# Turning half of one batch's heads by DMA instead of TensorE, and two small edits at the start, in a fused attention and GeGLU kernel

## Chip, cores, metric

One core of one Trainium2 chip. The metric is the device time of one execution in microseconds (us). The runs of one kernel in one job lay within 0.2 to 1.0% of each other; medians and ranges are given.

## The reference, cut to what matters

Inputs and output are float32; the kernel computes in bf16.

```python
B, H, S, Nb, D = 8, 8, 576, 16, 64
k_all = concat([beacon_k, k], axis=2); v_all = concat([beacon_v, v], axis=2)   # 592 keys
scores = q @ k_all.T / sqrt(D), causal over the 576, the 16 beacons always seen
attn   = softmax(scores) @ v_all
x = attn.transpose(0, 2, 1, 3).reshape(4608, 512)
out = (gelu(x @ w_gate) * (x @ w_val)) @ w_out        # d_ff = 1536
```

## The kernel before

It works batch by batch. Its score matmuls read queries and keys with the head dimension on the partitions (the tile `qkT`, one slot for each of four head pairs), while the inputs have tokens in rows, so it turns every batch. There are two ways in the kernel:

- **Packed and turned on TensorE** (batches 0 and 1): a load puts six consecutive tokens of a head into one partition (`qk6`), and 25 small transposes per head pair turn them.
- **Token rows and turned by DMA** (batches 2 to 7): the loads put one token into one partition (`q_sb`, `k_sb`), and ten DMA transposes, issued by SyncE, write `qkT`. TensorE does nothing for them.

All loads into bf16 tiles are issued by GpSimd and cast on the way. GpSimd also makes the causal masks of batches 1 to 7. It takes loads and masks in the order of the program: in the changed kernel batch 1's first mask starts at 60.20 us, behind the loads ahead of it, and at 48.86 with those loads moved (changed_q2_loads_later).

```python
    def load_qk6(b, h0, h1, ws=(1, 0)):                 # packed
        for w in ws:
            src = (q, k)[w]
            dma(qk6_of(b)[0][0:96, w, h0:h1, :],
                src[b, h0:h1, :, :].rearrange("h (p r) d -> p h (r d)", r=6))

    def transpose_pe(b, m, by_act=False):               # packed, on TensorE
        t_ps = psum_s.tile([P, 2, 1024], BF16, name="t_ps", tag="s")
        for w in range(2):
            tr_part(b, m, w, t_ps[:, w, :])             # 12 transposes, and 1 for the beacons
        ...                                             # copies to qkT

    def transpose_half(b, m, w, by_act=False):          # batch 0: q and k in two PSUM tiles
        ...
        if by_act:
            act(out_ap, in_ap, ACT.Copy)
        else:
            keep(nc.vector.tensor_copy(out_ap, in_ap))

    def transpose_dma(b):                               # token rows, by DMA
        q_sb, k_sb = q_ring[b % NRING], k_ring[b % NRING]
        for j in range(5):
            for w, src, n, c in (...q..., ...k...):
                keep(nc.sync.dma_start_transpose(
                    out=qkT[:, :, w, c + j * P : c + j * P + n],
                    in_=src[0:n, j, :, :].rearrange("p h d -> p (h d)")))
    # [cut]
    load_qk6(1, 0, 4)                                   # the order of the loads
    load_kb(1)
    load_gate_val(8, 12)
    load_qk6(1, 4, H)
    for f0 in (0, 4, 8):
        load_out_w(f0, f0 + 4)
    load_v(1)
    loads = qk_loads(2)
    ...
    ahead(5)                                            # batch 2's queries: before batch 1's masks
    # [cut] batch 0's scores; then, per batch b >= 1:
            o(4)                                        # output matmuls of the batch before
            scores(b, (0, 0)); scores(b, (0, 2)); scores(b, (0, 1))
            o(5)
            if b == 1:
                transpose_pe(1, 3)
            ahead(2)                                    # two loads, between masks
            o(4)
            scores(b, (0, 3), (1, 3)); scores(b, (1, 0)); scores(b, (1, 2))
            ahead(2)
            o(5)
            av(b, 0)                                    # attend: values of pair 0
```

The softmax here doesn't subtract the row's maximum and nothing guards it: scores larger than these inputs give would overflow.

## Time and profile before

| what | value |
|---|---|
| time, median of four runs | 369.48 us (368.95 to 369.69) |
| TensorE busy, granted clock | 97% of the span, 0.999 |
| third output-weight load landed | 45.53 us |
| last value load of batch 1 landed | 49.51 us |
| first gate matmul of batch 0, of batch 1 | 21.99 and 65.40 us: a stage of 43.41 us |

The landings are read off the trace, each DMA from the start of its issue to the semaphore update that tells of its landing.

The page of the kernel before. First come the span and the busy time of each engine, then rows of 40 equal slices of the span (a digit is the busy share in tenths), and engine shares of the chain that ended last.

```profile
span 367.6 us, 7553 instructions
PE 356.4 (97%) x3046; PEld 182.5 (50%) x3096; DVE 150.7 (41%) x256; ACT 188.1 (51%) x243; POOL 159.3 (43%) x282
PE   7799999999999999999999999999999999999996
PEclk9999999999999999999999999999999999999999
DMA  7999999999299915993399929992791130000112
PE 88%; DMA 5%; ACT 2%; issue 2%; POOL 1%; DVE 1%; ACTq 0%; POOLq 0%
```

PE (TensorE) is full (97%) and at full clock (0.999). But for the first quarter of the span the DMA engines are full as well: slices 2 to 10, up to about 90 us, are all 9. Up to 49.5 us they are busy with loads that batches 0 and 1 need.

The timeline of PE before, with start, length, instruction group and, in brackets, the idle time before it and what ended it.

```profile
16.61 0.27 PE L172 MATMUL s_ps<-qkT 64*128 64x208 bf16 x2 [0.41 <-ACT expT L175]
41.79 0.70 PE L180 MATMUL t_ps<-eye,qk 96*64 96x96 bf16 x24
46.04 1.02 PE L172 MATMUL o_ps<-wo_sb,hT_sb 128*128 128x512 bf16 x4
48.90 0.70 PE L180 MATMUL t_ps<-eye,qk 96*64 96x96 bf16 x24
51.61 1.25 PE L172 MATMUL o_ps<-wo_sb,hT_sb 128*128 128x512 bf16 x5
52.70 1.08 PE L172 MATMUL x_ps<-v_sb,expT 128*128 128x65 bf16 x30
```

The two groups of 24 transposes (41.79 and 48.90) are what the change takes away. Output matmuls (`o_ps`) and the first attend of batch 1 (softmax weights times values, `x_ps` at 52.70) start without a wait: the weights and the values were there, the latter with 3.2 us to spare.

The timeline of GpSimd (POOL) before, around batch 1's first masks.

```profile
45.81 3.31 POOL L108 DMA_DIRECT2D q_sb<-in_q_dram  x4 [1.67 <-DMA wo_sb<-in_moe_w_out_dram]
49.10 0.77 POOL L298 TENSOR_SCALAR_AFFINE_SELECT expT<-expT 128x224 bf16<-128x224 bf16 x2
```

GpSimd waits for the landing of an output-weight load before it issues a query load of batch 2. In this trace a load that waits starts 0.3 us after the landing of the one eight places ahead of it: the last value load of batch 1 at 40.73 and the first two query loads of batch 2 at 43.27 and 45.81, after the three output-weight landings at 40.44, 42.98 and 45.53. The masks come behind these loads.

### The profile page before, as it was taken

To read this page: it belongs to the slowest core of one execution; us is meant where nothing else is said; L and a number is where in the kernel's file an instruction comes from. 1 tells how busy PE (TensorE), PEld (TensorE's weight loads), DVE (VectorE), ACT (ScalarE), POOL (GpSimd) and SP (SyncE) were. 2 spreads that over 40 slices of the span, in tenths; PEclk is the share of its full clock that TensorE was granted. 3 is DMA by queue.
4 is the path that set the end of the run, shared out by engine and by line. 5 is a ranking of instruction groups with operands and counts; after the bars stand their busy time and mean duration, and the time that the engine had idled before them with its cause. 6 is when DMAs were issued, how large, how long until landed. Compare 5 with 4: busy or idle time off the path is not lost.

```text
span 367.6 us, 7553 instructions
## 1 busy us (share of the span) xinstructions
PE 356.4 (97%) x3046; PEld 182.5 (50%) x3096; DVE 150.7 (41%) x256; ACT 188.1 (51%) x243; POOL 159.3 (43%) x282
## 2 busy tenths in 40 slices
PE   7799999999999999999999999999999999999996
PEld 7564445544554455444544455445544554444443
DVE  4454543543353334433443235433444254333322
ACT  3963578237743576348723873367534863321210
POOL 8934397942495247723684249504700430000000
PEclk9999999999999999999999999999999999999999
DMA  7999999999299915993399929992791130000112
GB/s 104 177 203 204 194 143 115 148 145 109 63 114 149 135 46 118 148 153 49 90 142 136 106 61 135 156 99 67 113 132 37 41 108 1 2 0 29 59 38 105
DMA packets 149858, 38.35 MB, mean 104 GB/s; under 512 B 136384, under 2 KB 145344, under 8 KB 149824
## 3 DMA queue, kind: packets, MB, share of 16 engines
q0 software_dynamic: 104848, 19.11, 69.1%
q1 hardware_dynamic: 44976, 18.76, 28.0%
q8 instruction: 24, 0.39, 0.4%
q14 instruction: 10, 0.08, 0.1%
HBM read 38.27 MB, written 9.44 MB: 130 GB/s over the span
## 4 chain that ended last, share of the span: by engine, by line
PE 88%; DMA 5%; ACT 2%; issue 2%; POOL 1%; DVE 1%; ACTq 0%; POOLq 0%
PE gv_ps L172 42%; PE o_ps L172 25%; PE x_ps L172 7%; PE s_ps L172 7%; DMA q_sb<-in_q_dram 3%; DMA qkT<-k_sb 2%; ACT expT L175 2%; PE y_ps L180 2%; PE v_ps L172 1%; PE g_ps L172 1%; PE t_ps L180 1%; PE w_ps L172 1%; POOL v_sb L108 1%; DVE qkT L217 0%; DVE qkT L199 0%
## 5 line engine op out<-in xcount | busy, mean ns | idle before, releaser
L175 ACT ACTIVATE ge_sb<-gv_ps 128x512 bf16<-128x512 f32 x101 | 59.4, 597 | 132.8 <-PE gv_ps L172 132.8
L423 DVE TENSOR_TENSOR hT_sb<-gv_ps,ge_sb 128x512 bf16<-128x512 f32 x101 | 69.1, 690 | 105.0 <-ACT ge_sb L175 102.6
L175 ACT ACTIVATE expT<-s_ps 128x960 bf16<-128x960 f32 (+3 forms) x112 | 99.7, 968 | 19.5 <-PE s_ps L172 18.4
L172 PE MATMUL gv_ps<-xT_sb,wg_sb 128*128 128x512 bf16 x400 | 107.8, 379 | 0.2
L172 PE MATMUL gv_ps<-xT_sb,wv_sb 128*128 128x512 bf16 x390 | 104.1, 379 | 0.4
L172 PE MATMUL o_ps<-wo_sb,hT_sb 128*128 128x512 bf16 (+2 forms) x413 | 100.7, 374 | 2.5 <-issue 1.3
L298 POOL TENSOR_SCALAR_AFFINE_SELECT expT<-expT 128x256 bf16<-128x256 bf16 (+2 forms) x140 | 51.7, 385 | 97.9 <-ACT expT L175 97.5
L172 PEld LDWEIGHTS <-wv_sb 128*128 128x128 bf16 x432 | 42.2, 98 | 50.7
L172 PEld LDWEIGHTS <-wg_sb 128*128 128x128 bf16 x432 | 41.1, 98 | 46.7
L172 PEld LDWEIGHTS <-hT_sb 128*128 128x128 bf16 x444 | 38.8, 98 | 43.4 <-issue 6.2
L442 DVE COPY o_sb<-o_ps 128x512 f32<-128x512 f32 (+2 forms) x37 | 25.0, 675 | 42.1 <-PE o_ps L172 42.0
L108 POOL DMA_DIRECT2D v_sb<-in_v_dram x40 | 33.7, 862 | 6.3 <-DMA wg_sb<-in_moe_w_gate_dram 2.4
L172 PEld LDWEIGHTS <-expT 128*128 128x128 bf16 (+1 forms) x960 | 32.5, 97 | 6.7 <-POOL expT L298 1.6
L172 PE MATMUL s_ps<-qkT 64*128 64x512 bf16 (+5 forms) x384 | 32.4, 281 | 3.3 <-DVE qkT L221 1.6
L108 POOL DMA_DIRECT2D k_sb<-in_k_dram x30 | 25.2, 842 | 22.1 <-DMA q_sb<-in_q_dram 15.1
L172 PE MATMUL x_ps<-v_sb,expT 128*128 128x65 bf16 x930 | 33.3, 194 | 0.0
L108 POOL DMA_DIRECT2D q_sb<-in_q_dram x30 | 25.3, 885 | 4.3 <-DMA wo_sb<-in_moe_w_out_dram 3.5
L349 DVE TENSOR_TENSOR y_sb<-x_ps,r_sb 128x640 bf16<-128x640 f32 x31 | 25.6, 824 | 1.3 <-DVE r_sb L347 0.3
L172 PEld LDWEIGHTS <-qkT 64*128 64x128 bf16 x384 | 14.0, 94 | 24.2 <-issue 15.7
L347 DVE RECIPROCAL r_sb<-x_ps 128x10 f32<-128x10 f32 x31 | 6.8, 221 | 36.6 <-PE x_ps L172 36.6
L382 DVE COPY xT_sb<-y_ps 128x576 bf16<-128x576 bf16 x15 | 6.9, 457 | 10.6 <-PE y_ps L180 10.6
L597 ACT ACT_TABLE_LOAD x7 | 9.0, 1283 | 0.1
(54 smaller groups left out, 124.2 us busy)
## 6 DMA issues: line engine op xcount, KB each, us to landing
out_dram<-o_sb SPq DMA_DIRECT2D x35, 256.0 KB, 2.2
v_sb<-in_v_dram POOLq DMA_DIRECT2D x24, 128.0 KB, 6.8
q_sb<-in_q_dram POOLq DMA_DIRECT2D x24, 128.0 KB, 9.3
k_sb<-in_k_dram POOLq DMA_DIRECT2D x18, 128.0 KB, 9.9
wo_sb<-in_moe_w_out_dram POOLq DMA_DIRECT2D x3, 512.0 KB, 14.8
wg_sb<-in_moe_w_gate_dram POOLq DMA_DIRECT2D x2, 512.0 KB, 11.9
wv_sb<-in_moe_w_val_dram POOLq DMA_DIRECT2D x2, 512.0 KB, 13.3
v_sb<-in_v_dram POOLq DMA_DIRECT2D x8, 112.0 KB, 4.7
```

Of the source, the lines that this page charges most:

```text
L108: keep(nc.gpsimd.dma_start(out=out_ap, in_=in_ap))
L172: keep(nc.tensor.matmul(out_ap, lhsT, rhs, start=start, stop=stop, **kw))
L175: keep(nc.scalar.activation(out_ap, in_ap, func, **kw))
L180: keep(nc.tensor.transpose(out_ap, in_ap, ident[0:n, 0:n]))
L298: nc.gpsimd.affine_select(out=d, in_=d, pattern=[[0, 2], [1, n]], compare_op=ALU.is_ge, fill=0.0, base=NB if t == 0 else 0, channel_multip ...
L347: keep(nc.vector.reciprocal(r, x[:, :, :, D:DV]))
L349: nc.vector.tensor_tensor(out=y_sb[:, :, h0:h1, :].rearrange("p j b d -> p b j d"), in0=x[:, :, :, 0:D], in1=r.to_broadcast([P, h1 - h0, 5 ...
L382: keep(nc.vector.tensor_copy(out_ap, y_ps[:, 0:S]))
L423: nc.vector.tensor_tensor(out=h_of[ci][:, fi, :], in0=gv_of.pop((ci, fi))[1], in1=ge_sb, op=ALU.mult)
L442: keep(nc.vector.tensor_copy(o_sb[:, ti, c0:c1], o_ps))
L597: keep(nc.scalar.preload_act_table_set(SET_GELU))
```

## The change

Three edits. (1) Heads 4-7 of batch 1 are loaded as token rows and turned by ten half-width DMA transposes, to take 50 transposes off the full TensorE. (2) In batch 0, the values of pair 0 go ahead of a score chunk that waits for a PSUM buffer (0.41 us at 16.61, ended by an exp). (3) The first query copy out of PSUM, which the first scores wait for, is split between ScalarE and VectorE.

```diff
-    def qk_loads(b):
+    def qk_loads(b, h0=0):                 # and key_loads: heads h0 to H alone
...
-                (q_sb[0:n, j, :, :], q[b, :, j * P : j * P + n, :].rearrange("h p d -> p h d"))
+                (q_sb[0:n, j, h0:H, :], q[b, h0:H, j * P : j * P + n, :].rearrange("h p d -> p h d"))
@@ transpose_half
+        t0 = 52 if by_act else 0
         if by_act:
-            act(out_ap, in_ap, ACT.Copy)
-        else:
-            keep(nc.vector.tensor_copy(out_ap, in_ap))
+            act(out_ap[:, 0:t0, :], in_ap[:, 0:t0, :], ACT.Copy)
+        keep(nc.vector.tensor_copy(out_ap[:, t0:, :], in_ap[:, t0:, :]))
@@ transpose_dma(b, m0=0)
-                        out=qkT[:, :, w, c + j * P : c + j * P + n],
-                        in_=src[0:n, j, :, :].rearrange("p h d -> p (h d)"),
+                        out=qkT[:, m0:NPAIR, w, c + j * P : c + j * P + n],
+                        in_=src[0:n, j, 2 * m0 : H, :].rearrange("p h d -> p (h d)"),
@@ loads
-    load_qk6(1, 4, H)
+    load_qk(1, 4)
@@ batch 0
+    av(0, 0, "ot")
     c((2, 3), (3, 3))
-    av(0, 0, "ot")
@@ batches
-            o(5)
-            if b == 1:
-                transpose_pe(1, 3)
             ahead(2)
-            o(4)
+            o(9)
...
-            if b == 0 and fi in (6, 7, 9):
-                transpose_pe(1, min(fi - 6, 2), by_act=True)
+            if b == 0 and fi in (6, 7):
+                transpose_pe(1, fi - 6)
...
-                if 2 <= b + 1 < B:
-                    transpose_dma(b + 1)
+                if b + 1 < B:
+                    transpose_dma(b + 1, 0 if b else 2)
```

More of the change, by code (lines that the diff above doesn't have):

```diff
@@ L129, in load_kb, with key_loads @@
         dma(qk6_of(b)[1], beacon_k[b].rearrange("h t d -> t h d"))
-    def key_loads(src, beacon, dst, b):
+    def key_loads(src, beacon, dst, b, h0=0):
+        dst, src, beacon = dst[:, :, h0:H, :], src[:, h0:H, :, :], beacon[:, h0:H, :, :]
         parts = [
@@ L147, in qk_loads, with load_qk @@
             parts.append(
-                (q_sb[0:n, j, :, :], q[b, :, j * P : j * P + n, :].rearrange("h p d -> p h d"))
+                (q_sb[0:n, j, h0:H, :], q[b, h0:H, j * P : j * P + n, :].rearrange("h p d -> p h d"))
             )
-        return [lambda o=o, i=i: dma(o, i) for o, i in parts] + key_loads(k, beacon_k, k_sb, b)
-    def load_qk(b):
-        for load in qk_loads(b):
+        return [lambda o=o, i=i: dma(o, i) for o, i in parts] + key_loads(k, beacon_k, k_sb, b, h0)
+    def load_qk(b, h0=0):
+        for load in qk_loads(b, h0):
             load()
@@ L191, in tr_part, with transpose_pe @@
             tr(dst[:, S:SK], kb[:, 2 * m : 2 * m + 2, :])
-    def transpose_pe(b, m, by_act=False):
+    def transpose_pe(b, m):
         t_ps = psum_s.tile([P, 2, 1024], BF16, name="t_ps", tag="s")
@@ L199, in transpose_pe @@
         keep(nc.vector.tensor_copy(out_ap[:, 1], in_ap[:, 1]))
-        if by_act:
-            act(out_ap[:, 0], in_ap[:, 0], ACT.Copy)
-        else:
-            keep(nc.vector.tensor_copy(out_ap[:, 0], in_ap[:, 0]))
+        act(out_ap[:, 0], in_ap[:, 0], ACT.Copy)
         keep(nc.vector.tensor_copy(qkT[:, m, 1, 0:NB], t_ps[:, 1, S:SK]))
@@ L213, in transpose_half @@
         in_ap = t_ps[:, 0:S].rearrange("p (r t) -> p t r", r=6)
+        t0 = 52 if by_act else 0
         if by_act:
-            act(out_ap, in_ap, ACT.Copy)
-        else:
-            keep(nc.vector.tensor_copy(out_ap, in_ap))
+            act(out_ap[:, 0:t0, :], in_ap[:, 0:t0, :], ACT.Copy)
+        keep(nc.vector.tensor_copy(out_ap[:, t0:, :], in_ap[:, t0:, :]))
         return t_ps
@@ L231, in warm, with transpose_dma @@
             mm(w_ps[:, 0, 0:D], idle[:, 0:P], idle[:, 0:D], True, True)
-    def transpose_dma(b):
+    def transpose_dma(b, m0=0):
         q_sb, k_sb = q_ring[b % NRING], k_ring[b % NRING]
```

## The prediction

> **What bounds it now.** TensorE: the page's first part has PE busy 356.4 of 367.6 us (97%) at granted clock 0.999; the chain of waits is 88% PE. Removed PE work counts unless PE then waits. The second limit is the DMA engines: the page's slices show them at nine tenths from 10 to 55 us. Landings, read off the DMA issues: gate/value weights finish at 34.97, batch 1 heads 4-7 (two loads) at 37.93, the three output-weight loads at 40.44, 42.98, 45.53, batch 1's values at 49.51. GpSimd issues them at most eight ahead, between its causal masks, in order.
>
> **What the change removes (timeline, PE).**
> - Transposes of pairs 2 and 3 of batch 1: 25 transposes each, 0.74 us plus about 0.1 us of joints (at 41.86 and 48.98): 1.6-1.8 us of PE.
> - Values of pair 0 move into the 0.41 us wait at 16.61 (PE on ACT's exp): 0.3-0.4 us, if exps stay back to back.
> - First query copy: ACT took 6.43-7.09, PE waited to 7.13, VectorE was free from 6.43. Half each: about 0.2 us.
> About 2.2 us, all on PE's path.
>
> **What it adds.**
> - Batch 1 heads 4-7 as token rows: 4672 pieces of 128 B. The trace moves such pieces at about 1200 per us (values of batch 1: 4608 in 3.8 us), so 3.9 us against 3.0: +1.0 us.
> - Eleven small loads instead of two, through an eight-deep window at 0.7-0.9 us of GpSimd issue each: an estimated 0.5-1 us bubble.
> - Ten DMA transposes from SyncE of half width. Between 112 and 126 us full-width ones held loads to under half their rate: an estimated 7.5 us of engine time per batch, so 3.7-4.3 us for half. SyncE issues them at about 1.2 us each, near 36 to 48 us. [...] the row loads fall from 1200 pieces/us to about 500 beside transposes.
>
> So the third output-weight load should land near 49-50 instead of 45.5, and batch 1's values near 54-55 instead of 49.5. PE, 1.4 us earlier, wants the former at about 47 and the values at about 50.4. Slack was about 3 us each; it is overrun. GpSimd, waiting to issue batch 2's queries behind these landings, starts batch 1's masks near 53 instead of 49.1 us, so the first attend of batch 1 ends near 56-57.5 instead of 53.6. The 2.2 us are swallowed and 2-4 us lost, once. Later batches just shift.
>
> **Prediction: 371.5 us**, 8 in 10: 366.8 to 374.8. Faster by over 2%: 0.01; within 2%: 0.94; slower by over 2%: 0.05. If DMA contention costs less than I think and nothing stalls, it is 367.2.
>
> **What would show it.** Right: PE idle of several us between 46 and 57 us, ended by the output weights' load, the values' load or masks; masks of batch 1 starting after 51; values of batch 1 landing after 53; exps starting 0.2 us sooner. Wrong: output weights landed by 47, values by 51, PE continuous from 45 to 65, PE busy down 1.7 us with the span down about 2.
>
> **What would make it wrong.** Half-width transposes costing far less engine time than half; a stall further on, where batch 1's xT turns (landed 64.61, wanted 65.56) slip too; qkT of pair 2 landing after PE wants it (about 53), which would add to the loss.

## The result, and the profile after

| | before | changed |
|---|---|---|
| time, median of four runs, us | 369.48 (368.95 to 369.69) | 380.57 (378.67 to 381.24) |
| TensorE busy, granted clock in the profiled run | 97%, 0.999 | 96%, 0.986 |
| third output-weight load landed | 45.53 | 55.33 |
| last value load of batch 1 landed | 49.51 | 61.51 |
| batch 1's first mask started | 49.10 | 60.20 |
| first attend of batch 1 ended | 53.8 | 64.4 |
| stage, gate matmul of batch 0 to that of batch 1 | 43.41 | 54.20 |

The ratio is 1.0294 (95% interval 1.0256 to 1.0333): slower. The profiled spans differ by 11.1 us, and the one stage by 10.8. The later stages take the same time in both (39.3 to 39.6 us each): the loss falls once, between 46 and 66 us.

The page after:

```profile
span 378.7 us, 7541 instructions
PE 362.4 (96%) x3046; PEld 182.4 (48%) x3046; DVE 149.1 (39%) x252; ACT 187.4 (49%) x242; POOL 166.0 (44%) x291
PE   7799947999999999999999999999999999999996
PEclk9999976999999999999999999999999999999999
PE 82%; DMA 12%; POOL 4%; issue 1%; DVE 0%; POOLq 0%; DVEq 0%
```

PE has a hole in its sixth and seventh slices, and in the same place the granted clock falls. The chain is 12% DMA instead of 5%. PE's total busy time went *up* although 50 transposes are gone: matmuls at half clock are busy for longer (four output matmuls 1.90 us instead of 1.02, below; some matmul records are missing from the trace of before, too, so the two totals are not compared further).

The timeline of PE after:

```profile
46.91 1.04 PE L173 MATMUL o_ps<-wo_sb,hT_sb 128*128 128x512 bf16 x4 [0.82 <-DMA wo_sb<-in_moe_w_out_dram]
50.36 1.02 PE L173 MATMUL o_ps<-wo_sb,hT_sb 128*128 128x512 bf16 x4 [1.69 <-DMA wo_sb<-in_moe_w_out_dram]
55.38 2.29 PE L173 MATMUL o_ps<-wo_sb,hT_sb 128*128 128x512 bf16 x5 [3.99 <-DMA wo_sb<-in_moe_w_out_dram]
60.66 1.09 PE L173 MATMUL x_ps<-v_sb,expT 128*128 128x65 bf16 x15 [0.24 <-POOL expT L296]
63.37 1.00 PE L173 MATMUL x_ps<-v_sb,expT 128*128 128x65 bf16 x15 [1.62 <-POOL expT L296]
64.18 1.90 PE L173 MATMUL o_ps<-wo_sb,hT_sb 128*128 128x512 bf16 x4
```

Each of the three output-weight loads is waited for (0.82, 1.69, 3.99 us), then the masks. The last line shows the half clock: four output matmuls take 1.90 us, where four took 1.02 at 46.04 before.

The timeline of GpSimd after:

```profile
50.60 0.88 POOL L108 DMA_DIRECT2D q_sb<-in_q_dram  x1 [2.72 <-DMA wo_sb<-in_moe_w_out_dram]
55.62 1.75 POOL L108 DMA_DIRECT2D q_sb<-in_q_dram  x2 [4.13 <-DMA wo_sb<-in_moe_w_out_dram]
60.20 1.38 POOL L296 TENSOR_SCALAR_AFFINE_SELECT expT<-expT 128x224 bf16<-128x224 bf16 x4
62.89 1.45 POOL L296 TENSOR_SCALAR_AFFINE_SELECT expT<-expT 128x256 bf16<-128x256 bf16 x4
```

GpSimd sits in front of query loads of batch 2, which nobody needs yet, until output weights have landed; the masks stand behind it.

Stretches of the kernel after, with the busy time of each engine, then the granted clock, the DMA share and GB/s:

```profile
46.90:55.40 8.50, 2.81 (x19) 1.16 (x20) 0.00 (x0) 2.98 (x4) 1.62 (x2) 0.84 1.41 149
55.40:59.50 4.10, 4.10 (x15) 1.24 (x15) 0.69 (x1) 1.33 (x2) 2.61 (x3) 0.50 2.77 142
59.50:62.90 3.40, 1.89 (x19) 0.81 (x17) 0.00 (x0) 1.28 (x2) 3.39 (x9) 1.00 2.20 202
62.90:66.30 3.40, 2.93 (x23) 1.44 (x25) 1.05 (x2) 0.00 (x0) 3.18 (x6) 0.50 1.51 98
```

PE is busy for 2.81 of 8.50 us, and the clock is 0.50 from 52.67 to 59.50 and from 62.91 to 66.32 (by the trace's clock records): stretches of 6.83 and 3.41 us. In the 3.42 us before the first PE was busy for 1.02, in the 3.41 us before the second for 1.89. With idle matmuls put ahead of these waits the clock stayed at 1.00 from 46 to 63.8 us (changed_pe_kept_busy). How busy PE has to be for that, no run here shows.

The start. All engines around the first query copy, before:

```profile
6.43 0.65 ACT L175 ACTIVATE qkT<-t_ps 128x576 bf16<-128x576 bf16 x1 [4.34 <-PE t_ps L180]
7.13 0.39 PE L172 MATMUL s_ps<-qkT 64*128 64x512 bf16 x2 [0.75 <-ACT qkT L175]
```

and after:

```profile
6.45 0.43 ACT L176 ACTIVATE qkT<-t_ps 128x312 bf16<-128x312 bf16 x1 [4.36 <-PE t_ps L181]
6.92 0.43 DVE L215 COPY qkT<-t_ps 128x264 bf16<-128x264 bf16 x1 [0.77 <-ACT qkT L176]
7.48 0.39 PE L173 MATMUL s_ps<-qkT 64*128 64x512 bf16 x2 [1.07 <-DVE qkT L219]
```

The halves do not run side by side. VectorE (DVE) starts its half when ScalarE (ACT) has ended, and PE's wait before the first scores grows from 0.75 to 1.07 us.

### The profile page after: what moved, and what is told of

Its sections match the earlier page's. It is cut to its first block, busy times and chain, and to the rows that moved or that the text cites. A ratio compares the mean times of both kernels' runs of the same rounds, so it can differ in the third digit from the quotient of the medians.

```text
span 378.7 us, 7541 instructions
## 1 busy us (share of the span) xinstructions
PE 362.4 (96%) x3046; PEld 182.4 (48%) x3046; DVE 149.1 (39%) x252; ACT 187.4 (49%) x242; POOL 166.0 (44%) x291
## 4 chain that ended last, share of the span: by engine, by line
PE 82%; DMA 12%; POOL 4%; issue 1%; DVE 0%; POOLq 0%; DVEq 0%
PE gv_ps L173 41%; PE o_ps L173 24%; PE x_ps L173 7%; PE s_ps L173 6%; DMA v_sb<-in_v_dram 4%; DMA wv_sb<-in_moe_w_val_dram 4%; DMA wg_sb<-in_moe_w_gate_dram 2%; DMA qk<-in_q_dram 2%; PE g_ps L173 1%; PE v_ps L173 1%; POOL k_sb L108 1%; PE y_ps L181 1%; POOL qk L108 1%; POOL wo_sb L108 1%; POOL expT L296 0%
## 5 line engine op out<-in xcount | busy, mean ns | idle before, releaser
L173 PE MATMUL o_ps<-wo_sb,hT_sb 128*128 128x512 bf16 (+2 forms) x444 | 108.2, 379 | 6.5 <-DMA wo_sb<-in_moe_w_out_dram 6.5
L173 PE MATMUL gv_ps<-xT_sb,wv_sb 128*128 128x512 bf16 x404 | 108.1, 379 | 0.0
L173 PEld LDWEIGHTS <-hT_sb 128*128 128x128 bf16 x444 | 39.3, 99 | 52.1 <-issue 14.2
L108 POOL DMA_DIRECT2D k_sb<-in_k_dram x35 | 28.8, 827 | 26.4 <-DMA q_sb<-in_q_dram 12.9
L173 PE MATMUL x_ps<-v_sb,expT 128*128 128x65 bf16 x930 | 34.2, 194 | 2.3 <-POOL expT L296 1.9
L108 POOL DMA_DIRECT2D q_sb<-in_q_dram x35 | 28.9, 855 | 14.3 <-DMA wo_sb<-in_moe_w_out_dram 6.9
## 6 DMA issues: line engine op xcount, KB each, us to landing
wo_sb<-in_moe_w_out_dram POOLq DMA_DIRECT2D x3, 512.0 KB, 10.1
```

The costliest lines, as they stand in the source:

```text
L108: keep(nc.gpsimd.dma_start(out=out_ap, in_=in_ap))
L173: keep(nc.tensor.matmul(out_ap, lhsT, rhs, start=start, stop=stop, **kw))
```

## The experiments

**Theory.** The DMA part of the change puts more on the DMA engines than they have room for before 53 us, by two separate costs: the eleven row loads with the gaps that their issue leaves, and the ten transposes. PE then waits, GpSimd's load-before-mask order adds to the wait, and the clock halves. **Rivals:** one of the two DMA costs is all of it; the row form itself is much more work for the engines; the small edits carry part of the loss; the order of the loads alone is at fault.

Fifteen kernels ran; each gave a correct result. In the table, W is the landing of the last gate/value weights (where the loads in question begin), O that of the third output-weight load, V that of batch 1's last values, and "stage" runs from the first gate matmul of batch 0 to that of batch 1. All are from each run's trace. The sections have the times of all runs.

| run | W | O | V | stage |
|---|---|---|---|---|
| before | 34.97 | 45.53 | 49.51 | 43.41 |
| changed | 36.35 | 55.33 | 61.51 | 54.20 |
| dma_part_alone | 34.83 | 54.24 | 59.91 | 53.55 |
| rows_turned_on_pe | 34.58 | 49.57 | 54.10 | 47.27 |
| rows_interleaved | 34.47 | 44.95 | 51.67 | 44.01 |
| ten_half_transposes_added | 35.54 | 47.96 | 57.16 | 49.39 |
| ten_full_transposes_added | 34.72 | 47.26 | 59.32 | 51.40 |
| half_transposes_early | 41.19 | 51.74 | 55.93 | 50.15 |
| changed_q2_loads_later | 35.26 | 53.65 | 59.52 | 52.07 |
| changed_rows_after_values | 34.78 | 42.41 | 46.66 | 52.92 |
| changed_pe_kept_busy | 35.78 | 54.04 | 61.46 | 50.88 |
| changed_repaired | 34.58 | 45.49 | 53.55 | 45.39 |

### dma_part_alone

The kernel before with edit (1) alone: the diff above without the two hunks "transpose_half" and "batch 0".

> The kernel before with the first part of the change alone: heads 4-7 of batch 1 loaded as token rows and turned by ten half-width DMA transposes. My theory (the extra DMA work of this part delays the output weights and batch 1's values, PE idles, the clock halves) expects all of the loss here: 378 to 382 us, third output-weight load landing near 55 us, last value load of batch 1 near 61. The rival that the two small edits of batch 0's start carry a good part of the loss expects under 376 us.

Measured: 378.93 us (378.38 to 380.08; before 369.90), ratio 1.0239 (1.0206 to 1.0273). O at 54.24, V at 59.91, the same two stretches of half clock (51.6 to 58.4 and 61.9 to 65.3). The stage is 10.1 of the changed kernel's 10.8 us longer than before's: the loss is this part's. The run met both expectations for O and V within about 1 us.

### small_parts_alone

```diff
+    av(0, 0, "ot")
     c((2, 3), (3, 3))
-    av(0, 0, "ot")
```
and the hunk "transpose_half" of the change.

> The kernel before with the two small edits alone: values of pair 0 ahead of the shared score chunk, and first query copy split over ScalarE and VectorE. My theory, after the trace: the split copy runs one half after the other (VectorE's half waited for ScalarE's), so it gains nothing and may lose 0.2 to 0.3 us, the other edit gains 0.2 to 0.4 us: within 0.5 us of before. The rival that the start costs something real expects +1 us or more (gate/value matmuls started 0.8 us later in the changed kernel).

Measured: 370.34 us (368.93 to 371.87), ratio 1.0006 (0.9974 to 1.0039), five rounds: not told from before. Its stage is 43.41, to the digit that of before. The changed kernel's gate matmuls had started 0.8 us later than before's; here they started 0.25 us earlier, so the small edits alone do not explain that delay. Most likely it was the luck of the first landings (in the changed kernel's profile PE also waits 0.72 us for a query load at 12.25), but that is not shown.

### rows_turned_on_pe

The row loads of edit (1) stay, the DMA transposes of this batch do not: TensorE turns the rows, in ten transposes per pair.

```diff
-    load_qk6(1, 4, H)
+    load_qk(1, 4)
+    def transpose_rows(b, m, by_act=False):
+        t_ps = psum_s.tile([P, 2, 1024], BF16, name="t_ps", tag="s")
+        for w, src in ((1, k_sb), (0, q_sb)):
+            for j in range(5):
+                n = P if j < 4 else (64, 80)[w]
+                tr(t_ps[:, w, j * P : j * P + n], src[0:n, j, 2 * m : 2 * m + 2, :].rearrange("p h d -> p (h d)"))
+        ...                                    # two copies to qkT, at the places of before
```

> The kernel before with heads 4-7 of batch 1 loaded as token rows (eleven loads instead of two), but still turned on TensorE, in 10 instead of 25 transposes per pair, and no DMA transposes for this batch. If the transposes by DMA cause the loss: third output-weight load 1 to 2 us later than before's 45.5, values of batch 1 by 51.5, no wait on PE, 368 to 370 us. If the eleven small row loads and their eight-deep window cause it: output weights past 50 and 375 us or more.

Measured: 373.99 us (372.82 to 375.25), ratio 1.0100 (1.0070 to 1.0130). It falls between the two expectations: the loads have a cost of their own, 4.1 us by the medians, and neither sole-cause theory holds. The row loads landed about where the prediction had put them (the last at 39.66), but the engines did not move them at full rate. The DMA view of this run between 35 and 39 us, as 40 slices, GB/s per slice and packets:

```profile
DMA  9999989988755999999975999999999999999999
GB/s 106 91 77 74 60 53 56 58 53 54 44 35 31 61 92 110 106 132 115 83 48 36 59 68 63 68 95 100 111 88 81 93 106 106 104 88 85 117 131 80
DMA packets 2607, 0.32 MB, mean 80 GB/s; under 512 B 2607, under 2 KB 2607, under 8 KB 2607
```

The busy digits hide it, for most are still 9; the packets show it. 2607 packets in 4 us are 650 per us, where 128 B pieces ran at 1198 per us with the loads back to back (5393 packets between 46 and 50.5 us of before, shown below). GpSimd needs about 0.74 us to issue such a load of 512 pieces (in before 0.54 us for one of 128, 0.88 for one of 1024, so most of it came per load and not per piece), and the engines moved one in 0.41 to 0.48 us (landings at 36.79, 37.27 and 37.68 us in the changed kernel). And the output weights behind the rows are issued at 37.7 instead of 26.7 us, so the first of them took 4.1 us after the rows, where 2.54 us is its pace in before.

GpSimd's order shows here too; the timeline of PE of this run:

```profile
49.61 0.38 PE L173 MATMUL o_ps<-wo_sb,hT_sb 128*128 128x512 bf16 x1 [1.29 <-DMA wo_sb<-in_moe_w_out_dram]
56.67 0.63 PE L173 MATMUL x_ps<-v_sb,expT 128*128 128x65 bf16 x15 [1.60 <-POOL expT L312]
```

The values had landed at 54.10; the second half of the attend waited until 56.67 for a mask.

### rows_interleaved

The same eleven row loads, set between the three output-weight loads; pairs 2 and 3 both turned on TensorE after the first five output matmuls of batch 1.

```diff
-    load_qk(1, 4)
-    for f0 in (0, 4, 8):
+    rows = qk_loads(1, 4)
+    for f0, r0, r1 in ((0, 0, 2), (4, 2, 5), (8, 5, 8)):
+        for load in rows[r0:r1]:
+            load()
         load_out_w(f0, f0 + 4)
+    for load in rows[8:]:
+        load()
```

> As rows_turned_on_pe, but the eleven row loads stand between the three output-weight loads (2, 3, 3 ahead of them, 3 after) instead of all ahead, and pairs 2 and 3 of batch 1 are both turned on TensorE in batch 1's first stretch. Same bytes, same number of loads. If the eleven loads cost time because GpSimd needs about 0.74 us to issue what the DMA engines move in 0.42 us (a gap, not work): the long loads fill the gap, the last values land by 52 instead of 54.1, and the time is about 371 to 372.5 us. If the row form itself is that much more DMA work: the last values land near 54 again, 373.5 us or more.

Measured: 372.38 us (370.31 to 373.40), ratio 1.0073 (1.0045 to 1.0102). V came to 51.67 as the gap theory said, O to 44.95, and the stage to 44.01, 0.6 us over before's. So an issue gap, not work, was most of what the rows cost the stage (3.3 of 3.9 us), and about half of what they cost V (2.4 of 4.6 us). The time by the rounds is 2.6 us over before's 369.75, more than the 0.65 us between the two profiled spans; the range of the runs is wide, and I leave that difference open.

### ten_half_transposes_added

The kernel before, plus ten half-width transposes that nobody needs, started by the landing of a weight tile at about 35 us.

```diff
+                if b == 0:
+                    for i in range(10):
+                        keep(nc.sync.dma_start_transpose(
+                            out=xT_sb[:, 0:2, 3328 + P * i : 3328 + P * (i + 1)],
+                            in_=wv_sb[:, i % 4, 1024 : 1024 + 2 * P]))
```

> The kernel before, with ten half-width DMA transposes added that nobody needs (of a weight tile that has just landed at about 35 us, into columns of xT that are written much later; the result stays right). Loads and PE work are those of before. If the transposes delay the loads by their presence alone: the third output-weight load and the values land 4 to 7 us later than before's 45.5 and 49.5, and the time is 373 to 377 us. If row loads or waits on them cause the loss: at most 1 us over before.

Measured: 375.99 us (375.55 to 376.84), ratio 1.0159 (1.0127 to 1.0191): within the theory's range for the time. The landings missed theirs (4 to 7 us): O was 2.4 us late, V 7.65. No row loads, no PE work removed, nobody waits for the transposes, and still V lands 7.65 us later. 0.57 of that is a later start (W), so the ten transposes took 7.1 us from the loads. The prediction had put 3.7 to 4.3. PE's two waits in this run, 2.14 and 1.65 us, are for GpSimd's masks, which stand behind loads that wait for the late landings; the clock then halves from 57.91 to 61.32.

Packets that the DMA engines moved between 46 and 50.5 us in before (all loads):

```profile
DMA packets 5393, 0.70 MB, mean 156 GB/s; under 512 B 5391, under 2 KB 5391, under 8 KB 5391
```

and in this run (1512 of the loads, 517 of the transposes):

```profile
DMA  9999999499999999999999999999990011101119
DMA packets 2030, 0.34 MB, mean 77 GB/s; under 512 B 2003, under 2 KB 2029, under 8 KB 2029
```

While weights of 1024 B pieces were loading, the transposes and the loads moved about as many packets each (for example 156 against 159 between 42 and 43 us; in the changed kernel 651 against 673 between 46 and 50.5 us). In the window above, where the loads were 128 B pieces, the whole traffic fell to under half of before's (77 against 156 GB/s). That is not so wherever the two meet: from 51 to 55 us, with both still under way, it was 136 GB/s. A part of the fall is a standstill. The DMA digits show 0 and 1 from 49.4 to 50.4 us, although value loads and transposes had been issued and not landed. The profiles of ten_full_transposes_added (near 48 us), half_transposes_early (near 33), dma_part_alone (near 52) and the changed kernel (near 53) show standstills of 0.5 to 1.2 us too; before and the two runs with rows turned on TensorE show none over 0.3 us between 34.5 us and V. What causes it, and why the rest of the window is slow, stays open.

### ten_full_transposes_added

`0:2` becomes `0:4` and `2 * P` becomes `4 * P` in the added lines.

> As ten_half_transposes_added, but the ten added DMA transposes are of full width (512 columns, twice the data). If the cost goes with the amount turned, as the prediction took it, the last value load of batch 1 lands about 7 us later than with half width (57.2), near 64, and the time is 381 to 384 us. If it goes with the number of transposes, it stays within 2 us of the half-width run's 376.0 us.

Measured: 377.46 us (376.38 to 378.33), ratio 1.0196 (1.0153 to 1.0239). V at 59.32: twice the data takes 10.1 us from the loads (V less W, against before) instead of 7.1. "In proportion to the data" is refuted: twice the data cost 1.4 times as much. So the prediction failed twice here: full width costs about 10, not the 7.5 that I had read from the stretch between 112 and 126 us, and half of the width does not cost half of that.

### half_transposes_early

As ten_half_transposes_added, from `wg_sb[:, i % 4, 0 : 2 * P]`, which lands at about 17 us, so that they meet loads in large pieces.

> The ten half-width transposes nobody needs, but of the first gate weights, so that they start near 17 us and meet loads that are written in pieces of 1024 B and 768 B, not the 128 B pieces of values and queries. If a transpose costs the same beside any load: everything after is 7 us late, as the values were in ten_half_transposes_added (57.2 against 49.5). If it costs less beside large pieces: batch 1's last query/key load lands 4 to 6 us later than before's 37.9.

Measured: 374.64 us (two runs, 373.31 and 375.97), ratio 1.0129 (1.0085 to 1.0173). The last query/key load of batch 1 landed at 43.83 instead of 37.93: 5.9 us, as the second case expected. So the transposes were at most somewhat cheaper beside large pieces, 0.59 against 0.71 us each. By V, which came 6.4 us later, the difference is smaller still. And it is near the spread of single profiles: W differs by 0.8 us between the two runs above, whose loads are the same until then. Even this is over what the prediction allowed.

### changed_q2_loads_later

```diff
-    ahead(5)
...                                  # the three places among batch 1's masks
-            ahead(2)
-            ahead(2)
-            ahead(2)
+                                     # first place: none
+            ahead(6)
+            ahead(5)
```

> The changed kernel, with the five query loads of batch 2 no longer issued by GpSimd ahead of batch 1's masks but after the masks of pair 1's second chunk (six, then five loads). In the changed kernel the masks began at 60.2 and the one of pair 0's last chunk at 62.9, while the last values landed at 61.5. If GpSimd's order adds to the loss: masks begin as soon as the scores are there (before 58.5), the first values of batch 1 end with the value load, near 62.5 instead of 64.3, and the time falls by 1 to 3 us. If only the landings matter: within 0.7 us of the changed kernel.

Measured: 378.47 us (377.52 to 379.28), ratio 1.0223 (1.0188 to 1.0258), so about 2 us better than the changed kernel's 1.0294 (the two intervals just touch). Its GpSimd timeline:

```profile
48.86 0.38 POOL L296 TENSOR_SCALAR_AFFINE_SELECT expT<-expT 128x224 bf16<-128x224 bf16 x1 [1.53 <-ACT expT L176]
```

The masks now start with the exps. The first attend ended 0.45 us after V (59.97 and 59.52), where it ended 2.9 us after V in the changed kernel (64.4 and 61.51): GpSimd's order was worth 2.4 us there. Not all of it is a gain. PE waits 1.75 us at 64.74 for a mask that now stands behind the moved loads, and V was itself 2 us earlier in this profile; the stage is 2.1 us shorter. The expectation for the time holds.

### changed_rows_after_values

The q2 edit above, and the row loads moved behind the output weights and batch 1's values.

```diff
-    load_qk(1, 4)
     for f0 in (0, 4, 8):
         load_out_w(f0, f0 + 4)
     load_v(1)
+    load_qk(1, 4)
```

> The changed kernel, with the output weights and batch 1's values loaded ahead of the token rows of heads 4-7, and batch 2's queries after the masks as in the run before this one. Output weights land by 43 and values by 48, so no wait there and masks from about 49. The transposes then start near 47 and end near 59, while PE wants pair 2 at about 53: a wait of 3 to 6 us moves to the scores of pair 2. I expect 371 to 376 us: better than the changed kernel, not better than before. If the order alone was the fault: 367 to 368.5.

Measured: 379.03 us (378.56 to 380.32), ratio 1.0244 (1.0209 to 1.0279). A miss on the size: O and V landed by 42.41 and 46.66, but PE then waited longer than the 3 to 6 us that I expected, in the scores of pair 2:

```profile
62.15 1.23 PE L173 MATMUL s_ps<-qkT 64*128 64x512 bf16 x4 [8.48 <-DMA qkT<-q_sb]
```

SyncE issued the ten transposes from 46.96 to 61.29, 14.3 us for the ten; the last query part that pair 2's scores read landed at 62.06. In and after this wait the clock halves too, from 56.16 to 66.40. Late rows only move the wait.

### changed_pe_kept_busy

Idle matmuls (`warm`) ahead of PE's waits in batch 1, in the changed kernel:

```diff
+            if b == 1:
+                warm(30)
+                o(4)
+                warm(130)
+                o(5)
+            else:
+                o(9)
...
+            if b == 1:
+                warm(60)
             av(b, 0)
```

> The changed kernel, with small idle matmuls put on TensorE before its waits (30 before the second, 130 before the third output-weight load, 60 before the first values of batch 1; their result is read by nobody). In the changed kernel the granted clock was 0.5 from 52.7 to 59.5 and from 62.9 to 66.3 us. If the halved clock after the wait is part of the loss: the clock stays at 1.0 (or nearly), and the time falls by 1 to 3 us from 380.6, most of it from the second stretch, since in the first PE waits for masks anyway. If not: no change, or a little slower.

Measured: 381.35 us (380.32 to 381.65), ratio 1.0296 (1.0263 to 1.0330): no gain in time. The clock did stay up:

```profile
46.00:57.30 11.30, 9.09 (x186) 6.62 (x186) 1.38 (x2) 5.20 (x6) 3.36 (x4) 1.00 2.01 149
57.30:63.80 6.50, 5.90 (x113) 4.02 (x112) 0.69 (x1) 2.62 (x3) 5.34 (x12) 1.00 2.58 173
```

and from the end of the first attend to batch 1's gate matmul it took 11.6 us, like before's 11.6, where the changed kernel took 12.6. So the halved clock costs about 1 us there. But the profiled run had half clock at the start instead (10.4 to 17.2 us) and gave 1.4 us back in later stages. The expectation of a faster run is refuted: the other three runs took 381.21 to 381.65 us too, at granted clocks of 0.986 to 0.996 (the changed kernel's four: 0.981 to 0.991). What the half clock costs in time is not shown beyond this 1 us in one stretch, and that the halved clock, which the theory counts, adds to the loss of the whole run is not shown.

### values_first_alone, split_copy_alone, split_from_two_tiles

One small edit each. The third makes the query transposes twice, into two PSUM tiles, one for each engine:

```diff
+        if by_act:
+            t2_ps = psum_s.tile([P, 2, 1024], BF16, name="t2_ps", tag="s")[:, 0, :]
+            tr_part(b, m, w, t2_ps)
...
+            in2_ap = t2_ps[:, 0:S].rearrange("p (r t) -> p t r", r=6)
+            act(out_ap[:, 0:52, :], in_ap[:, 0:52, :], ACT.Copy)
+            keep(nc.vector.tensor_copy(out_ap[:, 52:, :], in2_ap[:, 52:, :]))
```

> The kernel before with the values of batch 0's pair 0 ahead of the shared score chunk, nothing else. Expected: TensorE's 0.41 us wait at 16.6 us is filled, and a shorter wait of about 0.3 us follows before the next values, since ScalarE's exps end no sooner: 0 to 0.3 us faster, below what the rounds can tell. This is also the only candidate for a version that beats both.

> The kernel before with the first query copy split over ScalarE and VectorE, nothing else. Expected, after the trace: VectorE's half starts when ScalarE's has ended, and the first scores start 0.3 us later after the end of their transposes than in before (a wait of 1.07 instead of 0.75 us): 0.3 us slower, which the rounds can hardly tell. If the split helped as predicted: the wait shrinks to 0.55 us.

> The split copy again, but with the query transposes made twice, into two PSUM tiles, so that ScalarE and VectorE read different tiles (12 more transposes on TensorE, about 0.35 us). If the second half waits because both read one PSUM tile: VectorE's half now waits for TensorE alone and runs beside ScalarE's, and the wait before the first scores is under 0.75 us. If it waits because both write one tile: the halves stay one after the other, near 1.07 us.

Measured: values first, 370.80 us (369.40 to 371.49), ratio 1.0018 (0.9997 to 1.0039); the 0.41 us wait is gone and one of 0.30 us stands before the next attend (at 19.52), as expected, but no gain can be told. Split copy, 370.54 us (370.09 to 372.27), ratio 1.0022 (1.0001 to 1.0044), with the wait of 1.07 us: nothing gained, if anything lost. Split from two tiles (one look, 369.20 us, its state unknown):

```profile
6.22 0.43 ACT L175 ACTIVATE qkT<-t_ps 128x312 bf16<-128x312 bf16 x1 [4.13 <-PE t_ps L180]
6.47 0.43 DVE L220 COPY qkT<-t_ps 128x264 bf16<-128x264 bf16 x1 [0.33 <-PE t_ps L180]
7.04 0.39 PE L172 MATMUL s_ps<-qkT 64*128 64x512 bf16 x2 [0.61 <-DVE qkT L226]
```

VectorE now waits for PE alone, and runs beside ScalarE from 6.47 to 6.65. So the halves went one after the other from one tile (in the changed kernel ScalarE from 6.45 for 0.43 us, VectorE from 6.92), and side by side from two. What it is in the shared tile that made the wait, the runs do not tell.

### changed_repaired

The changed kernel with all repairs found: no split copy, rows interleaved as in rows_interleaved, queries of batch 2 later.

> The changed kernel without the split copy, with its eleven row loads set between the output-weight loads and batch 2's query loads after the masks: the two repairs found, and only the ten DMA transposes left of the loss. If the causes add up (rows and their gap 3 to 4 us, GpSimd's order 2 us, transposes 6 us): 374 to 377 us, still slower than before. If the transposes cost only because of the gap and the order: 368 to 370 us.

Measured: 373.94 us (372.98 to 374.42), ratio 1.0107 (1.0081 to 1.0133), just below the theory's range. The stage is 45.39, 2.0 us over before's although two groups of transposes are gone from PE: V lands at 53.55, and PE waits 1.7 us for values and 1.7 us for `qkT` of pair 2. It gives 1.5 us more back in the next stage (40.79 instead of 39.31), where gate matmuls wait 1.31 us for a piece of xT whose DMA took 7.4 us. Repairs return 8.8 of the 10.8 us; what remains keeps the change slower.

### two_small_repaired

The one version that the runs pointed to: before, with the values first and the split from two tiles.

> The kernel before with the values of pair 0 ahead of the shared chunk and the split copy made from two PSUM tiles: the only version that the runs point to as better than both. Expected gain 0.1 to 0.4 us of TensorE waits at the start, 369.0 to 369.6 against 369.5; the rounds will most likely not tell it from before.

Measured: 369.59 us (369.25 to 370.38), ratio 0.9997 (0.9975 to 1.0019): not told from before, and 2.9% below the changed kernel by the medians. No version here beats before beyond doubt.

## Why the prediction was wrong

It named the way of the loss and got its size wrong: 2 us expected in the median, 11.1 measured.

- **Right: the place and the chain.** PE idle between 46 and 63 us (the prediction had said 57), ended by output weights and masks; one-off loss; later stages the same.
- **Right: what PE saves.** From batch 0's first gate matmul to its first output matmul before took 24.05 us (21.99 to 46.04); the changed kernel took 24.14, of which 0.82 is a wait, so 23.32: one group of transposes was worth 0.73 us of its 0.8 to 0.9.
- **Wrong: "7.5 us of engine time per batch, so 3.7-4.3 us for half".** Measured alone, 7.1 us for ten half-width transposes and 10.1 for full width: about 3 us too little. This is one of the two terms that failed. I had taken it from a stretch where I could not see what the loads would have done without the transposes, and scaled it by data.
- **Wrong: row loads "+1.0 us" and "an estimated 0.5-1 us bubble".** Measured alone, V was 4.6 us later, not 1.5 to 2: the second term that failed, again by about 3 us. Interleaved, so that long loads fill the gap, it was 2.2 us later, near the sum that I had put. The gap was what I had wrong: the small loads drained faster (0.41 to 0.48 us) than GpSimd issued them (0.74 us), and the large loads behind them start late (37.7 instead of 26.7 us). I had counted only the gap among the small loads.
- **Mis-sized by these: GpSimd's masks, "near 53".** They started at 60.20 because the landings that GpSimd waits for were late. The order itself was worth 2.4 us at the first attend.
- **Missing: the half clock.** I expected several us of idle PE and did not ask what that does to the clock: 0.50 for 6.83 and 3.41 us. It was about 1 us after the first attend; in the stretch before it, the attend had to wait for masks anyway.
- **Wrong: the split copy, "half each: about 0.2 us".** It added 0.3 us of waiting: the halves ran one after the other while both engines read one PSUM tile. The rounds cannot tell so little.
- **Half right: values ahead of the shared chunk, "0.3-0.4 us".** The wait of 0.41 us goes, one of 0.30 comes; the ends of ScalarE's exps set the pace.

The two DMA costs add up: stages 3.9 us (rows_turned_on_pe) and 6.0 us (ten_half_transposes_added) longer than before make 9.8; dma_part_alone is 10.1 longer. The agreement is partly luck: the first two keep transposes on TensorE that the third does not have, and V, counted from W, came 5.0, 7.1 and 10.5 us later, so that by the landings the parts overlap.

One thing stays open: why the DMA engines' whole traffic falls to less than half (77 against 156 GB/s), with a standstill of about 1 us in it, in one stretch where transposes meet 128 B pieces.

## What to carry to other kernels

Before work is moved from a full engine to DMA, look at the DMA engines in that very stretch: here the loads were back to back, and ten added transposes brought the last values 7.65 us later. The price of a DMA transpose should be measured by adding some that nobody needs, since it went neither with data (7.1 us for ten of half width, 10.1 for full) nor with a reading from another stretch (7.5). Small loads that GpSimd issued slower than they drained (0.74 against 0.41 to 0.48 us) left gaps; set such loads between long ones (the last values came at 51.67 instead of 54.10 us), and put loads that are not yet needed behind the work that is (2.4 us at the first attend). And a PSUM copy split over two engines ran side by side only from two tiles (from 6.47 to 6.65); what that is worth in time, the rounds could not tell.
